# A linear-attention and gated feed-forward kernel: weight loads in three groups, casts moved to GpSimd, a product in two steps, and a new order of the first stage

## The chip, the cores and the metric

The kernel runs on one core of a Trainium2 chip. The metric is the device time of one launch in microseconds (us), median over runs. The engines are TensorE (PE, with its weight loads listed as PEld), VectorE (DVE), ScalarE (ACT), GpSimd (POOL) and SyncE (SP). Here SP issues the loads of the inputs and the stores of the output, GpSimd issues the loads of the weights.

## The reference, cut to what matters

Two operations follow each other. The first is a recurrence over 768 time steps for 4 batches and 8 heads of 48 channels; the second normalises each of the 3072 tokens and applies a gated feed-forward layer with 1536 hidden units.

```python
for t in range(S):                       # S = 768, per batch b and head h
    cur = einsum('bhd,bhe->bhde', u * k_t, v_t)
    y[:, :, t] = einsum('bhd,bhde->bhe', r_t, state + cur)
    state = w_t[..., None] * state + einsum('bhd,bhe->bhde', k_t, v_t)
x = y.transpose(0, 2, 1, 3).reshape(B * S, H * D)        # 3072 x 384
xn = x / sqrt(mean(x * x) + 1e-6) * rms_g
out = (silu(xn @ w_gate) * (xn @ w_val)) @ w_out
```

All inputs and the output are float32. The term with `u` contributes (sum over d of r u k) times v to y; the kernel calls it the bonus.

## The kernel before, in words

Time is cut into 6 superblocks n = 0 to 5 of 128 steps, and in each the 4 batches j = 0 to 3 are handled as blocks of 128 x 384. The recurrence is done in chunks: logarithms of w (`ln`) are summed by a matmul with a triangular matrix (`cs_mm`), exponentials of the sums (`exp_r`, `exp_k`) scale r and k (`r_mul`, `k_mul`) into the tile `rk`; `rk` is transposed (`rk_pe` or a transposing DMA, then `rk_tr`), the products of r and k within the chunk are formed (`q_mm`) and masked (`q_mask_e`, `q_mask_o`), and multiplied with v (`y_mm`), which needs v in bf16 (`cast_v`, tile `vb`). The state is carried by `st_mm` and `st_new` (tile `st`). The bonus runs beside it: `bonus_mul` on GpSimd (r x k x u, two products), `bonus_sum` on VectorE (the sum over a head's channels, tile `diag`), `bonus_v` on GpSimd (times v, tile `ydiag`). In superblock 0 `x_pe` adds `ydiag` into the bank of `y_mm` with a matmul. Then `x_sq`, `x_rstd` and `xn_mul` normalise on ScalarE, `xn_pe` transposes, and `xn_out` on VectorE multiplies by `rms_g` (tile `gT`) into `xnt`.

The feed-forward stage of superblock n works on all 512 tokens at once: for each of 12 blocks f of hidden units, `gate_mm` and `val_mm` (three matmuls of 512 columns each, tiles `wg_sb` and `wv_sb`), `silu` on ScalarE, `h_mul` on VectorE, and finally `o_mm` per batch, `o_out` and `out_dma`. `gate_mm.0.0` is the first such step; it needs all four `xn_out.0.j`.

Every step has a name of the form function.superblock.index. The order is written out by hand in the string `ORDER`: the program calls the functions in that order, so each engine, and each DMA queue, gets its instructions in the order in which their steps stand. An engine works strictly in that order; where a step waits, all behind it on that engine wait. Semaphores between engines follow from the tiles.

The PSUM banks are taken from three rings: "a" (2 banks: sums of `cs_mm`, `gate_mm`), "b" (2 banks: the second sums, `val_mm`), and "q" (4 banks, everything else). `val_mm` thus can't start before the `h_mul` of the value product two before it has read its bank.

In the first stage TensorE has little to do. 13 matmuls on a tile of zeros at the start and 36 steps `warm` among the others fill its time; nothing reads their results. Superblocks 0 and 1 share one load of w (`WIN`). The weights of gate and value are loaded by GpSimd's queue in two groups, hidden blocks 0 to 3 and 4 to 11:

```python
GV = (0, 4, 12)
CAST_ACT = sel("00 01 02 03 10 11 12 13")     # cast_v on ScalarE, else on GpSimd
```

The two products of `bonus_mul` (L467, L468), the casts (L379 on ScalarE, L381 on GpSimd), the weight loads (L351), `xn_out` (L607), the products `r_mul` (L455) and `k_mul` (L461), and the feed-forward products (L626) are the lines that matter below. In superblock 1, `r_mul` and `k_mul` read both operands from SBUF tiles (`er`, `ek`), in superblock 0 one of them from PSUM.

Of the kernel before, what the change touches and what calls it, by code (L numbers as in the profile page):

```python
# [25 lines left out]
load_w.0.1 load_r.0.0 load_w.0.0 warm.4.0 warm.18.0 load_r.0.1 load_k.0.1 load_w.0.2 load_k.0.0 ln.0.1 load_k.0.2  # L26
load_w.0.3 ln.0.0 load_r.0.2 warm.31.0 load_v.0.0 load_v.0.1 warm.22.0 load_k.0.3 load_r.0.3 load_v.0.3 load_v.0.2
cs_mm.0.1 exp_r.0.1 exp_k.0.1 cs_mm.0.0 load_r.1.1 load_k.1.0 load_r.1.0 load_k.1.1 w_tot.0.1 ln.0.2 warm.10.0
load_r.1.3 load_k.1.3 load_r.1.2 load_k.1.2 r_mul.0.1 load_v.1.0 load_v.1.1 load_v.1.2 exp_k.0.0 bonus_mul.0.1
load_v.1.3 load_w.2.0 warm.7.0 exp_r.0.0 k_mul.0.1 bonus_mul.0.0 rk_pe.0.1 w_tot.0.0 warm.2.0 warm.21.0 load_w.2.1  # L30
rk_tr.0.1 warm.9.0 cs_mm.0.2 warm.27.0 bonus_sum.0.1 exp_r.0.2 r_mul.0.0 k_mul.0.0 bonus_mul.0.2 warm.12.0 warm.34.0
warm.13.0 ln.0.3 r_mul.0.2 warm.26.0 rk_pe.0.0 exp_k.0.2 warm.5.0 rk_tr.0.0 load_r.2.1 load_w.2.2 warm.19.0 warm.32.0
cast_v.0.0 cs_mm.0.3 load_r.2.0 load_k.2.0 q_mm.0.1 warm.8.0 w_tot.0.2 k_mul.0.2 bonus_sum.0.0 exp_k.0.3 cs_mm.1.0
bonus_v.0.1 q_mm.0.0 exp_r.0.3 exp_k.1.0 q_mask_e.0.1 q_mask_o.0.1 bonus_sum.0.2 k_mul.0.3 exp_r.1.0 w_tot.0.3
r_mul.0.3 warm.24.0 warm.29.0 rk_pe.0.2 warm.1.0 x_pe.0.1 cast_v.0.1 rk_tr.0.2 y_mm.0.1 bonus_v.0.0 bonus_mul.0.3
q_mask_o.0.0 rk_pe.0.3 q_mask_e.0.0 q_mm.0.2 x_pe.0.0 x_sq.0.1 cast_v.0.3 rk_tr.0.3 q_mask_o.0.2 load_gv.0.0
bonus_sum.0.3 q_mask_e.0.2 cs_mm.1.1 x_rstd.0.1 q_mm.0.3 warm.17.0 bonus_v.0.2 q_mask_o.0.3 y_mm.0.0 warm.25.0
exp_r.1.1 load_w.2.3 x_pe.0.2 load_k.2.1 cast_v.0.2 bonus_v.0.3 warm.20.0 x_sq.0.0 y_mm.0.2 st_mm.0.0 warm.6.0
warm.35.0 xn_mul.0.1 x_rstd.0.0 x_sq.0.2 warm.15.0 q_mask_e.0.3 warm.23.0 x_pe.0.3 xn_mul.0.0 warm.3.0 warm.16.0
y_mm.0.3 exp_k.1.1 cs_mm.1.3 k_mul.1.0 xn_pe.0.1 warm.0.0 bonus_mul.1.0 load_gv.0.1 load_gv.1.0 x_rstd.0.2 warm.30.0  # L40
x_sq.0.3 xn_mul.0.2 r_mul.1.1 st_new.0.0 xn_pe.0.0 r_mul.1.0 warm.14.0 x_rstd.0.3 warm.28.0 warm.33.0 xn_pe.0.2
xn_out.0.1 bonus_mul.1.1 warm.11.0 xn_mul.0.3 exp_k.1.3 xn_out.0.0 st_mm.0.3 xn_out.0.2 st_mm.0.2 xn_pe.0.3 exp_r.1.3
st_new.0.3 cs_mm.1.2 rk_pe.1.0 xn_out.0.3 k_mul.1.1 st_mm.0.1 st_new.0.1 k_mul.1.3 gate_mm.0.0 exp_r.1.2 bonus_sum.1.0
exp_k.1.2 rk_pe.1.1 gate_mm.0.3 rk_tr.1.0 val_mm.0.0 silu.0.0 bonus_sum.1.1 load_gv.1.1 load_r.2.2 bonus_mul.1.3
silu.0.3 val_mm.0.2 rk_tr.1.1 h_mul.0.0 gate_mm.0.2 st_new.0.2 silu.0.2 gate_mm.0.1 bonus_sum.1.3 val_mm.0.3
gate_mm.0.9 silu.0.1 h_mul.0.2 val_mm.0.1 gate_mm.0.6 silu.0.9 r_mul.1.3 h_mul.0.3 q_mm.1.0 h_mul.0.1 silu.0.6
q_mask_e.1.0 q_copy_o.1.0 q_mask_o.1.0 gate_mm.0.11 gate_mm.0.7 q_copy_o.1.1 silu.0.7 rk_pe.1.3 q_mask_e.1.1
q_mask_o.1.1 r_mul.1.2 bonus_v.1.0 val_mm.0.6 val_mm.0.7 cast_v.1.0 k_mul.1.2 rk_tr.1.3 gate_mm.0.5 h_mul.0.6 y_mm.1.0
load_wo.0.0 val_mm.0.9 silu.0.11 bonus_v.1.1 cast_v.1.2 load_wo.1.0 st_mm.1.0 cast_v.1.1 gate_mm.0.4 rk_pe.1.2
h_mul.0.7 st_mm.1.1 silu.0.5 val_mm.0.5 x_add.1.0 rk_tr.1.2 h_mul.0.9 cast_v.1.3 gate_mm.0.10 bonus_mul.1.2 val_mm.0.4  # L50
st_new.1.0 st_new.1.1 load_wo.2.0 q_mm.1.2 h_mul.0.5 silu.0.4 x_sq.1.0 h_mul.0.4 gate_mm.0.8 bonus_v.1.3 q_copy_o.1.3
x_rstd.1.0 q_mask_e.1.3 q_copy_o.1.2 val_mm.0.8 silu.0.8 val_mm.0.11 y_mm.1.1 silu.0.10 q_mask_e.1.2 bonus_sum.1.2
q_mask_o.1.3 h_mul.0.8 x_add.1.1 y_mm.1.3 st_mm.1.2 load_v.2.1 ln.2.0 st_mm.1.3 q_mask_o.1.2 val_mm.0.10 y_mm.1.2
x_sq.1.1 xn_mul.1.0 bonus_v.1.2 cs_mm.2.0 x_add.1.3 x_sq.1.3 st_new.1.2 h_mul.0.11 ln.2.1 h_mul.0.10 x_add.1.2
cs_add.2.0 o_mm.0.0 o_out.0.0 x_rstd.1.1 x_sq.1.2 xn_pe.1.0 xn_out.1.0 xn_mul.1.1 exp_r.2.0 st_new.1.3 cs_mm.2.1
cs_add.2.1 x_rstd.1.2 load_r.2.3 r_mul.2.0 o_mm.0.2 xn_pe.1.1 xn_mul.1.2 xn_pe.1.2 x_rstd.1.3 o_mm.0.1 xn_mul.1.3
bonus_mul.2.0 xn_out.1.1 exp_k.2.0 out_dma.0.0 load_k.2.2 exp_r.2.1 w_tot.2.0 load_v.2.0 ln.2.2 k_mul.2.0 ln.2.3
w_tot.2.1 r_mul.2.1 cs_mm.2.2 xn_pe.1.3 cs_mm.2.3 exp_k.2.1 xn_out.1.2 cs_add.2.2 k_mul.2.1 cs_add.2.3 cast_v.2.1
exp_r.2.2 exp_r.2.3 rk_tr.2.1 xn_out.1.3 o_mm.0.3 exp_k.2.3 o_out.0.1 w_tot.2.2 r_mul.2.2 bonus_mul.2.1 gate_mm.1.7
val_mm.1.7 exp_k.2.2 load_k.2.3 st_mm.2.1 rk_tr.2.0 bonus_sum.2.0 r_mul.2.3 w_tot.2.3 gate_mm.1.1 load_v.2.2 st_new.2.1  # L60
k_mul.2.2 silu.1.7 bonus_mul.2.2 silu.1.1 bonus_sum.2.1 val_mm.1.1 h_mul.1.7 gate_mm.1.6 silu.1.6 bonus_v.2.1
gate_mm.1.5 cast_v.2.0 k_mul.2.3 silu.1.5 rk_tr.2.2 val_mm.1.5 load_w.3.3 o_out.0.2 h_mul.1.1 gate_mm.1.3 gate_mm.1.0
val_mm.1.0 h_mul.1.5 o_out.0.3 silu.1.0 val_mm.1.6 q_mm.2.0 load_v.2.3 q_copy_o.2.0 silu.1.3 q_mask_o.2.0 gate_mm.1.2
st_mm.2.0 h_mul.1.0 val_mm.1.3 rk_tr.2.3 h_mul.1.6 load_w.3.1 load_w.3.0 gate_mm.1.10 val_mm.1.2 load_k.3.1
q_mask_e.2.1 silu.1.2 st_new.2.0 gate_mm.1.4 q_copy_o.2.1 cast_v.2.2 silu.1.4 q_mask_o.2.1 h_mul.1.3 q_mask_e.2.0
y_mm.2.1 y_mm.2.0 h_mul.1.2 st_mm.2.2 bonus_v.2.0 silu.1.10 x_add.2.1 x_add.2.0 gate_mm.1.9 val_mm.1.4 x_sq.2.1
gate_mm.1.8 val_mm.1.9 bonus_mul.2.3 st_new.2.2 out_dma.0.1 x_sq.2.0 h_mul.1.4 load_v.3.2 x_rstd.2.0 silu.1.9 silu.1.8
q_mm.2.2 bonus_sum.2.2 q_copy_o.2.2 h_mul.1.9 gate_mm.1.11 q_copy_o.2.3 out_dma.0.2 load_w.3.2 cast_v.2.3 bonus_v.2.2
bonus_sum.2.3 q_mask_o.2.3 st_mm.2.3 load_k.3.0 q_mask_o.2.2 q_mask_e.2.3 val_mm.1.11 q_mask_e.2.2 val_mm.1.10
bonus_v.2.3 y_mm.2.3 silu.1.11 y_mm.2.2 ln.3.0 h_mul.1.11 h_mul.1.10 x_rstd.2.1 x_add.2.2 ln.3.1 val_mm.1.8 ln.3.3  # L70
h_mul.1.8 cs_mm.3.0 load_r.3.0 x_sq.2.2 xn_mul.2.0 cast_v.3.2 cs_add.3.0 x_add.2.3 exp_k.3.0 x_sq.2.3 o_mm.1.0
cs_mm.3.1 xn_pe.2.0 exp_r.3.0 ln.3.2 x_rstd.2.2 o_mm.1.1 st_new.2.3 load_r.3.1 out_dma.0.3 w_tot.3.0 r_mul.3.0
xn_mul.2.1 k_mul.3.0 xn_mul.2.2 cs_add.3.1 exp_k.3.1 xn_pe.2.2 cs_mm.3.3 x_rstd.2.3 o_out.1.0 exp_r.3.1 bonus_mul.3.1
xn_out.2.2 xn_mul.2.3 o_mm.1.3 w_tot.3.1 xn_pe.2.3 o_out.1.1 cs_add.3.3 r_mul.3.1 load_k.3.2 load_r.3.3 xn_pe.2.1
xn_out.2.0 exp_r.3.3 exp_k.3.3 cs_mm.3.2 xn_out.2.3 o_mm.1.2 load_r.3.2 k_mul.3.1 w_tot.3.3 rk_tr.3.0 r_mul.3.3
cs_add.3.2 out_dma.1.0 xn_out.2.1 load_v.3.0 exp_r.3.2 gate_mm.2.5 exp_k.3.2 r_mul.3.2 w_tot.3.2 val_mm.2.0 gate_mm.2.0
bonus_mul.3.0 bonus_mul.3.2 k_mul.3.2 o_out.1.3 bonus_sum.3.0 silu.2.5 rk_tr.3.1 load_k.3.3 o_out.1.2 q_mm.3.0 silu.2.0
q_mask_e.3.0 val_mm.2.1 bonus_v.3.0 h_mul.2.0 gate_mm.2.1 load_w.4.1 load_v.3.1 load_k.4.3 st_mm.3.2 k_mul.3.3
q_copy_o.3.0 silu.2.1 rk_tr.3.2 load_v.4.0 rk_tr.3.3 val_mm.2.5 gate_mm.2.11 load_k.4.0 bonus_sum.3.1 cast_v.3.0
out_dma.1.1 load_v.3.3 load_w.5.2 q_mask_e.3.1 q_copy_o.3.1 gate_mm.2.2 silu.2.11 h_mul.2.5 val_mm.2.2 h_mul.2.1  # L80
load_w.4.0 gate_mm.2.3 load_v.4.1 silu.2.2 q_mask_o.3.0 cast_v.3.1 load_r.4.1 bonus_sum.3.2 h_mul.2.2 bonus_v.3.1
gate_mm.2.6 val_mm.2.3 y_mm.3.0 st_new.3.2 st_mm.3.0 silu.2.3 gate_mm.2.4 h_mul.2.3 silu.2.6 q_mask_o.3.1 st_new.3.0
st_mm.3.1 silu.2.4 x_add.3.0 load_k.4.1 gate_mm.2.7 val_mm.2.4 x_sq.3.0 gate_mm.2.10 out_dma.1.2 cast_v.4.0 st_new.3.1
val_mm.2.6 q_mm.3.2 h_mul.2.4 bonus_mul.3.3 h_mul.2.6 silu.2.7 val_mm.2.7 val_mm.2.10 load_w.4.3 x_rstd.3.0 silu.2.10
# [640 lines left out]
```

## Time and profile before

| | |
|---|---|
| median of 3 runs | 199.82 us |
| lowest, highest | 199.66, 200.43 us |
| span of the profiled execution | 199.4 us |
| PE, DVE, ACT, POOL busy in it | 194.7, 151.5, 137.1, 125.7 us |
| first feed-forward product (gate_mm.0.0) starts | 31.30 us |
| bytes by DMA, mean rate | 32.41 MB, 163 GB/s |

The profiled execution's own time is its span; the runs' times were taken without a profile and hold 0.4 us more at the median. In the profile a line such as L626 is the line of the kernel that issued an instruction; a row of a timeline has start and duration in us, engine, line, operation, output and inputs, and in brackets how long the engine was idle before it and what ended that. A matmul's duration includes the way through the array, so that successive matmuls overlap; the distance of their starts is what they cost. Busy time of PE includes the filling matmuls. DMA rows give the time from issue to landing.

### The profile page before, as it was taken

The numbers are of one execution on the slowest core, as the hardware profiler recorded it, in microseconds if no ns is written. First come the engines' busy times: TensorE is split into PE (matmuls) and PEld (weight loads), VectorE is DVE, ScalarE is ACT, GpSimd is POOL, SyncE is SP. The second block draws the span as 40 slices with busy tenths as digits, with TensorE's granted clock in tenths as the row PEclk, the third lists the DMA queues.
The fourth block names the chain that finished last, engine by engine and source line by source line (L and its number), as shares of the span: only waits on it lengthen the run. The fifth ranks groups of instructions, "written<-read, shape, count | busy, mean of one in ns | idle before, by whom it ended". The sixth has DMA issues, their size and how long they took to land.

```text
span 199.4 us, 4410 instructions
## 1 busy us (share of the span) xinstructions
PE 194.7 (98%) x1577; PEld 115.6 (58%) x1577; DVE 151.5 (76%) x290; ACT 137.1 (69%) x279; POOL 125.7 (63%) x184
## 2 busy tenths in 40 slices
...
GB/s 147 265 229 191 169 206 208 201 207 191 203 173 212 204 191 227 217 191 191 177 175 226 214 203 215 179 174 139 122 190 219 0 24 60 2 116 82 0 59 100
DMA packets 121566, 32.41 MB, mean 163 GB/s; under 512 B 116420, under 2 KB 120392, under 8 KB 121544
## 3 DMA queue, kind: packets, MB, share of 16 engines
...
q8 instruction: 12, 0.20, 0.4%
...
q10 hardware_dynamic: 8, 0.00, 0.0%
...
## 4 chain that ended last, share of the span: by engine, by line
PE 88%; DMA 5%; DVE 2%; POOL 2%; issue 1%; ACT 0%
PE ps_bu L626 12%; PE ps_av L626 12%; PE ps_au L626 11%; PE ps_bv L626 11%; PE ps_qu L672 7%; PE ps_qz L672 7%; DMA wg_sb<-in_moe_w_gate_dram 5%; PE ps_qx L672 5%; PE ps_qv L672 5%; PE ps_qz L502 1%; PE ps_qx L552 1%; PE ps_qv L502 1%; PE ps_qv L333 1%; PE ps_qu L285 1%; PE ps_qu L502 1%
## 5 line engine op out<-in xcount | busy, mean ns | idle before, releaser
L672 PEld LDWEIGHTS <-ht 128*128 128x128 bf16 x300 | 28.2, 98 | 16.6
L626 PEld LDWEIGHTS <-wg_sb 128*128 128x128 bf16 x216 | 23.1, 114 | 19.8 <-DMA wg_sb<-in_moe_w_gate_dram 0.9
L626 PEld LDWEIGHTS <-wv_sb 128*128 128x128 bf16 x216 | 23.0, 114 | 18.3
L658 DVE TENSOR_TENSOR ht<-ps_bv,sg 128x512 bf16<-128x512 f32 x35 | 24.0, 687 | 10.2 <-PE ps_bv L626 9.1
L658 DVE TENSOR_TENSOR ht<-ps_bu,sg 128x512 bf16<-128x512 f32 x37 | 25.4, 687 | 6.9 <-PE ps_bu L626 5.8
L235 ACT ACTIVATE sg<-ps_av 128x512 bf16<-128x512 f32 x37 | 22.0, 596 | 12.2 <-PE ps_av L626 11.6
L626 PE MATMUL ps_av<-xnt,wg_sb 128*128 128x512 bf16 x111 | 30.1, 380 | 0.0
L626 PE MATMUL ps_bu<-xnt,wv_sb 128*128 128x512 bf16 x111 | 30.1, 380 | 0.0
L626 PE MATMUL ps_au<-xnt,wg_sb 128*128 128x512 bf16 x105 | 28.5, 380 | 0.5 <-DMA wg_sb<-in_moe_w_gate_dram 0.5
L626 PE MATMUL ps_bv<-xnt,wv_sb 128*128 128x512 bf16 x105 | 28.5, 380 | 0.0
L235 ACT ACTIVATE sg<-ps_au 128x512 bf16<-128x512 f32 x35 | 21.0, 600 | 10.5 <-PE ps_au L626 8.7
L467 POOL TENSOR_TENSOR ruk<-rt,kt 128x384 f32<-128x384 f32 x24 | 24.0, 1001 | 6.1 <-DMA kt<-in_k_dram 5.2
L468 POOL TENSOR_TENSOR ruk<-ruk,u_bc 128x384 f32<-128x384 f32 x24 | 24.7, 1030 | 1.9
L520 POOL TENSOR_SCALAR_AFFINE_SELECT qts<-qts 128x512 bf16<-128x512 bf16 x20 | 12.8, 650 | 15.1 <-ACT qts L513 14.6
L477 POOL TENSOR_TENSOR ydiag<-vt,diag 128x384 f32<-128x384 f32 x24 | 20.2, 843 | 1.7 <-DVE diag L472 1.6
L461 POOL TENSOR_TENSOR rk<-kt,ek 128x384 bf16<-128x384 f32 x16 | 15.9, 1004 | 2.3 <-ACT ek L235 2.3
L672 PE MATMUL ps_qu<-wo_sb,ht 128*128 128x384 bf16 (+1 forms) x96 | 15.0, 306 | 0.0
L672 PE MATMUL ps_qz<-wo_sb,ht 128*128 128x384 bf16 x84 | 14.8, 326 | 0.0
L233 ACT ACT_TABLE_LOAD x10 | 12.8, 1283 | 1.8 <-PEq L709 1.6
L472 DVE TENSOR_REDUCE diag<-ruk 128x8 f32<-128x384 f32 x24 | 13.0, 543 | 0.2 <-POOL ruk L468 0.2
L235 ACT ACTIVATE lw<-wt 128x384 bf16<-128x384 f32 (+1 forms) x20 | 11.1, 577 | 2.6 <-DMA wt<-in_w_dram 2.6
L585 ACT ACTIVATE xn<-xb,rstd 128x384 bf16<-128x384 f32 x20 | 11.8, 603 | 0.8 <-POOL rstd L580 0.7
...
## 6 DMA issues: line engine op xcount, KB each, us to landing
rt<-in_r_dram SPq DMA_DIRECT2D x24, 192.0 KB, 4.0
kt<-in_k_dram SPq DMA_DIRECT2D x24, 192.0 KB, 4.2
vt<-in_v_dram SPq DMA_DIRECT2D x24, 192.0 KB, 4.0
out_dram<-ob SPq DMA_DIRECT2D x23, 192.0 KB, 2.3
wt<-in_w_dram SPq DMA_DIRECT2D x16, 192.0 KB, 4.0
wt<-in_w_dram SPq DMA_DIRECT2D x4, 384.0 KB, 4.4
wo_sb<-in_moe_w_out_dram POOLq DMA_DIRECT2D x3, 384.0 KB, 7.0
wg_sb<-in_moe_w_gate_dram POOLq DMA_DIRECT2D x1, 768.0 KB, 10.3
```

What stands on the lines that cost most here:

```text
L233: nc.scalar.preload_act_table_set(table_name)
L235: return nc.scalar.activation(**kw).ins
L461: eng.tensor_tensor(out=rk[:, n % 2, j, 1, :, 0:D], in0=inp["k", n, j], in1=bank["cs_k", n, j][:, 0:DM].rearrange("p (h d) -> p h d", h=H) ...
L467: nc.gpsimd.tensor_tensor(out=ruk[n, j], in0=inp["r", n, j], in1=inp["k", n, j], op=ALU.mult)
L468: nc.gpsimd.tensor_tensor(out=ruk[n, j], in0=ruk[n, j], in1=u_bc, op=ALU.mult)
L472: nc.vector.tensor_reduce(out=diag[n, j].rearrange("p h o -> p (h o)"), in_=ruk[n, j], axis=mybir.AxisListType.X, op=ALU.add)
L477: nc.gpsimd.tensor_tensor(out=ydiag[n, j], in0=inp["v", n, j], in1=diag[n, j].to_broadcast([128, H, D]), op=ALU.mult)
L520: nc.gpsimd.affine_select(out=qts[n, j][:, 1], in_=qts[n, j][:, 1], compare_op=ALU.is_gt, fill=0.0, base=0, pattern=[[0, NP], [1, 128]], c ...
L585: nc.scalar.activation(out=xn, in_=xb[n, j], func=AF.Copy, scale=rstd[n, j][:, 1, c:c + 1])
L626: nc.tensor.matmul(ps[:, cols], lhsT=units(ws, c, f), rhs=xnt[n][:, c, cols], start=(first and c == 0), stop=(c == KC - 1))
L658: nc.vector.tensor_tensor(out=ht[n][:, f, :], in0=bank.pop(("v", n, f)), in1=bank.pop(("sg", n, f)), op=ALU.mult)
L672: nc.tensor.matmul(ps[:, cols], lhsT=ht[n][:, f, b * L:(b + 1) * L], rhs=wo_sb[:, f, cols], start=(f == 0), stop=(f == FC - 1))
```

## The change

It has five parts.

- The weights of gate and value come in three groups of 4 hidden blocks each (`GV = (0, 4, 8, 12)`), six loads instead of four, on the same queue.
- `cast_v` of superblock 0 runs on GpSimd instead of ScalarE.
- `bonus_mul` multiplies r by u first and then by k. The first product is a function `bonus_u`, which in superblock 0 is a step of its own.
- The fill of `st` with zeros is left out. The matmul that spreads u over the partitions and the one that transposes `rms_g` become steps (`u_mm`, `u_out`, `g_mm`, `g_out`) and can be placed.
- The order is new, up to about the fourth superblock; the last 106 steps of PE, 96 of DVE, 110 of ACT, 57 of POOL and 43 of SP are as they were.

Dictionaries for split products (`PARTS`) and for waits between loads (`BEHIND`) are added and left empty.

```diff
-    CAST_ACT = sel("00 01 02 03 10 11 12 13")
+    CAST_ACT = sel("10 11 12 13")
...
     st = persist.tile([128, 2, SB, NP, 2 * D], BF16)
-    nc.vector.memset(st, 0.0)
...
-    GV = (0, 4, 12)
+    GV = (0, 4, 8, 12)
...
+    def u_mm(n, j):
+        bank["u", n, j] = psum("q", ("u", n, j), [128, DM])
+        nc.tensor.matmul(bank["u", n, j], lhsT=ones_row, rhs=u_row, start=True, stop=True)
+
+    def u_out(n, j):
+        nc.vector.tensor_copy(out=u_bc.rearrange("p h d -> p (h d)"), in_=bank.pop(("u", n, j)))
...
+    def bonus_u(n, j):
+        ruk[n, j] = pt.tile([128, H, D], FP32, name="ruk", bufs=NRUK)
+        nc.gpsimd.tensor_tensor(out=ruk[n, j], in0=inp["r", n, j], in1=u_bc, op=ALU.mult)
+
     def bonus_mul(n, j):
-        ruk[n, j] = pt.tile([128, H, D], FP32, name="ruk", bufs=NRUK)
-        nc.gpsimd.tensor_tensor(out=ruk[n, j], in0=inp["r", n, j], in1=inp["k", n, j], op=ALU.mult)
-        nc.gpsimd.tensor_tensor(out=ruk[n, j], in0=ruk[n, j], in1=u_bc, op=ALU.mult)
+        if (n, j) not in ruk:
+            bonus_u(n, j)
+        nc.gpsimd.tensor_tensor(out=ruk[n, j], in0=ruk[n, j], in1=inp["k", n, j], op=ALU.mult)
```

The order of the first stage, per engine, before (-) and after (+):

```diff
 SP
-load_w.0.1 load_r.0.0 load_w.0.0 load_r.0.1 load_k.0.1 load_w.0.2 load_k.0.0 load_k.0.2 load_w.0.3 load_r.0.2 load_v.0.0 load_v.0.1 load_k.0.3 load_r.0.3 load_v.0.3 load_v.0.2 load_r.1.1 load_k.1.0 load_r.1.0 load_k.1.1 load_r.1.3 load_k.1.3 load_r.1.2 load_k.1.2
+load_r.0.0 load_w.0.1 load_w.0.0 load_k.0.1 load_r.0.1 load_w.0.2 load_k.0.2 load_w.0.3 load_k.0.0 load_r.0.2 load_v.0.0 load_v.0.1 load_k.0.3 load_r.0.3 load_r.1.1 load_k.1.0 load_v.0.3 load_v.0.2 load_k.1.3 load_r.1.0 load_k.1.1 load_r.1.3 load_r.1.2 load_k.1.2
 POOL
-bonus_mul.0.1 bonus_mul.0.0 bonus_mul.0.2 bonus_v.0.1 bonus_v.0.0 bonus_mul.0.3 load_gv.0.0 bonus_v.0.2 bonus_v.0.3 bonus_mul.1.0 load_gv.0.1 load_gv.1.0 bonus_mul.1.1 load_gv.1.1 bonus_mul.1.3
+bonus_u.0.1 bonus_u.0.0 bonus_mul.0.1 bonus_mul.0.0 bonus_u.0.2 bonus_mul.0.2 bonus_v.0.1 bonus_v.0.0 cast_v.0.0 bonus_u.0.3 bonus_mul.0.3 cast_v.0.1 load_gv.0.0 bonus_v.0.3 bonus_v.0.2 cast_v.0.3 cast_v.0.2 load_gv.0.1 bonus_mul.1.0 load_gv.1.0 load_gv.2.0 bonus_mul.1.1 load_gv.1.1 load_gv.2.1 bonus_mul.1.3
 DVE, around xn_out of superblock 0
-q_mask_e.0.3 k_mul.1.0 r_mul.1.1 st_new.0.0 r_mul.1.0 xn_out.0.1 xn_out.0.0 xn_out.0.2 st_new.0.3 xn_out.0.3 k_mul.1.1 st_new.0.1 k_mul.1.3 bonus_sum.1.0 bonus_sum.1.1 h_mul.0.0 st_new.0.2 bonus_sum.1.3 h_mul.0.2
+q_mask_e.0.3 r_mul.1.1 st_new.0.0 r_mul.1.0 bonus_sum.1.0 xn_out.0.1 xn_out.0.0 xn_out.0.2 st_new.0.3 xn_out.0.3 k_mul.1.1 st_new.0.2 bonus_sum.1.1 r_mul.1.3 k_mul.1.3 st_new.0.1 h_mul.0.0 bonus_sum.1.3 h_mul.0.2
 PE, around the first feed-forward products
-xn_pe.0.2 warm.11.0 st_mm.0.3 st_mm.0.2 xn_pe.0.3 cs_mm.1.2 rk_pe.1.0 st_mm.0.1 gate_mm.0.0 rk_pe.1.1 gate_mm.0.3 val_mm.0.0 val_mm.0.2 gate_mm.0.2 gate_mm.0.1 val_mm.0.3 gate_mm.0.9 val_mm.0.1
+xn_pe.0.2 cs_mm.1.3 st_mm.0.3 warm.28.0 xn_pe.0.3 rk_pe.1.0 cs_mm.1.2 warm.33.0 st_mm.0.2 st_mm.0.1 gate_mm.0.0 val_mm.0.2 gate_mm.0.3 val_mm.0.0 warm.21.0 rk_pe.1.1 gate_mm.0.2 gate_mm.0.1 warm.11.0 gate_mm.0.9 val_mm.0.3 val_mm.0.1
 PE, the start
-warm.4.0 warm.18.0 warm.31.0 warm.22.0 cs_mm.0.1 cs_mm.0.0
+u_mm.0.0 warm.18.0 warm.2.0 warm.10.0 warm.8.0 warm.31.0 g_mm.0.0 warm.4.0 warm.22.0 cs_mm.0.1 warm.5.0 cs_mm.0.0
```

284 lines of the change are left out of this document (139 added, 145 removed).

## Prediction

> **What bounds the kernel now.** I read the page's engine table first, then busy time by stage, then the chain of waits, then each engine's timeline from 0 to 42 us, then the DMA views. The stage table (columns: stretch in us, PE, PEld, DVE, ACT and POOL busy, granted clock, DMA share, GB/s):
>
> ```profile
> PE 194.7 (98%) x1577; PEld 115.6 (58%) x1577; DVE 151.5 (76%) x290; ACT 137.1 (69%) x279; POOL 125.7 (63%) x184
> ...
> 0.00:31.30 31.30, 30.09 (x257) 18.17 (x258) 21.84 (x46) 22.38 (x50) 22.71 (x34) 1.00 1.00 202
> 31.30:37.00 5.70, 5.23 (x33) 2.79 (x31) 5.28 (x10) 5.25 (x8) 1.37 (x2) 1.00 1.13 204
> 37.00:196.40 159.40, 159.40 (x1291) 94.61 (x1291) 124.33 (x236) 109.11 (x222) 101.57 (x149) 1.00 0.74 155
> ```
>
> From 37 us to the last product TensorE has no gap. The reordering there can open a gap; it has none to close. What can be won lies ahead of 37 us, where busy time deceives, because `warm` matmuls fill it. The real mark is T, the start of gate_mm.0.0, the first product of the feed-forward stage. TensorE's timeline around it:
>
> ```profile
> 29.98 0.49 PE L402 MATMUL ps_av<-lw,mw 128*128 128x384 bf16 x2
> 30.30 0.49 PE L409 MATMUL ps_bu<-lw,mw 128*128 128x384 bf16 x2
> 30.63 0.61 PE L484 MATMUL ps_qz<-ident,rk 128*128 128x128 bf16 x8
> 31.08 0.33 PE L530 MATMUL ps_qu<-vb,rk 128*128 128x96 bf16 x4
> 31.30 0.81 PE L626 MATMUL ps_au<-xnt,wg_sb 128*128 128x512 bf16 x3
> ...
> 36.92 0.84 PE L626 MATMUL ps_au<-xnt,wg_sb 128*128 128x512 bf16 x3 [0.47 <-DMA wg_sb<-in_moe_w_gate_dram]
> ```
>
> T is 31.30 now, and 5 us later TensorE waits 0.47 us for the second gate group. TensorE's real work ahead of T consists of the same steps in both orders (all of superblock 0, cs_mm.1.0 to 1.3, rk_pe.1.0), so also what follows. Hence: new time = old time + (new T - 31.30) + fillers behind T - 0.47 + new waits behind T.
>
> T itself hangs on xn_out, on VectorE. VectorE's timeline:
>
> ```profile
> 7.00 0.56 DVE L334 COPY u_bc<-ps_qv 128x384 f32<-128x384 f32 x1 [2.41 <-PE ps_qv L333]
> 7.48 0.15 DVE L337 COPY gT<-ps_qx 128x3 f32<-128x3 f32 x1
> ...
> 24.45 0.55 DVE L461 TENSOR_TENSOR rk<-kt,ek 128x384 bf16<-128x384 f32 x1
> 24.91 1.35 DVE L455 TENSOR_TENSOR rk<-rt,er 128x384 bf16<-128x384 f32 x1
> ...
> 26.66 2.18 DVE L455 TENSOR_TENSOR rk<-rt,er 128x384 bf16<-128x384 f32 x1
> 28.75 0.55 DVE L607 TENSOR_TENSOR xnt<-ps_qu,gT 128x384 bf16<-128x384 bf16 x1
> 29.22 0.54 DVE L607 TENSOR_TENSOR xnt<-ps_qv,gT 128x384 bf16<-128x384 bf16 x1
> ```
>
> The product r_mul of superblock 1 takes 0.55 us at its cheapest sister (24.45) and 1.35 or 2.18 where GpSimd works beside it; the 2.18 pushes xn_out.0.1 to 28.75. GpSimd's timeline shows what ran beside it:
>
> ```profile
> 13.82 1.00 POOL L467 TENSOR_TENSOR ruk<-rt,kt 128x384 f32<-128x384 f32 x1 [0.92 <-DMA rt<-in_r_dram]
> 14.90 1.00 POOL L468 TENSOR_TENSOR ruk<-ruk,u_bc 128x384 f32<-128x384 f32 x1
> 15.86 0.83 POOL L477 TENSOR_TENSOR ydiag<-vt,diag 128x384 f32<-128x384 f32 x1
> ...
> 24.51 1.34 POOL L468 TENSOR_TENSOR ruk<-ruk,u_bc 128x384 f32<-128x384 f32 x1
> 25.80 0.81 POOL L351 DMA_DIRECT2D wv_sb<-in_moe_w_val_dram  x1
> 26.60 0.77 POOL L351 DMA_DIRECT2D wg_sb<-in_moe_w_gate_dram  x1
> 27.40 1.01 POOL L467 TENSOR_TENSOR ruk<-rt,kt 128x384 f32<-128x384 f32 x1
> ```
>
> **The change part by part.** *State fill.* It goes from VectorE, which sat idle 2.41 us behind it (row 7.00); worth nothing. u_mm and g_mm become steps; g_out moves behind k_mul.0.0, 0.15 us (row 7.48), with no reader before xn_out.0.1.
>
> *Casts.* The four casts of superblock 0 leave ScalarE and join GpSimd:
>
> ```profile
> 16.68 0.52 ACT L379 CAST vb<-vt 128x384 bf16<-128x384 f32 x1
> ...
> 28.45 0.58 ACT L585 ACTIVATE xn<-ps_bu,rstd 128x384 bf16<-128x384 f32 x1
> ```
>
> ```profile
> L381 POOL CAST vb<-vt 128x384 bf16<-128x384 f32 x16 | 8.0, 503 | 0.6 <-DMA vt<-in_v_dram 0.6
> ```
>
> ScalarE sheds 4 x 0.52 = 2.1 us ahead of its last xn_mul (28.45). It keeps only part: on SP load_k.0.0 falls from seventh to ninth place, so k_mul.0.0 and rk_tr.0.0 come later. k.0.0 arrives 2 places later, nearly 2 us at 202 GB/s, and the waiting ScalarE regains part of that; I estimate that 0.8 of the 2.1 us is kept: xn_mul.0.3 ends at 28.2 instead of 29.03.
>
> *Bonus product in steps.* GpSimd's work per block stays two products; r x u can start before k is there. That helps only at the very beginning, where bonus_mul.0.0 then waits for k.0.0. r.0.2 is tenth on SP in both orders with the same bytes ahead, and lands at 13.82 (row); k.0.0, one 192 KB load ahead at 202 GB/s, lands 1.0 earlier: 12.85. From there GpSimd has no gap up to load_gv.0.1. In its new order, pitches from the rows (independent product 0.96, dependent 1.08, bonus_v 0.83, cast 0.50, issue 0.81 to 1.0): bonus_mul.0.0 0.96, bonus .0.2 2.04, two bonus_v 1.66, cast 0.50, bonus .0.3 2.04, cast 0.50, load_gv.0.0 1.0, two bonus_v 1.66, two casts 1.0, load_gv.0.1 0.81: 12.2 us, to 25.05.
>
> Two more moves I price at nothing. Three more fillers stand ahead of cs_mm.0.1 and delay the first exponentials, but k_mul.0.0 waits for k.0.0 anyway; without that cover it is three fillers, 0.5 us at 0.16, on ScalarE's chain. load_v.0.3 and load_v.0.2 go two places back on SP, but GpSimd reads them only after load_gv.0.0, at 21.5.
>
> Then comes bonus_mul.1.0 (both steps), which needs r.1.0, the twentieth load on SP now, the nineteenth before. Issue times and landings of places 19 and 20:
>
> ```profile
> 19.23 0.81 SPq L248 DMA_DIRECT2D rt<-in_r_dram  x1
> 20.09 0.65 SPq L248 DMA_DIRECT2D kt<-in_k_dram  x1
> ```
>
> ```profile
> rt<-in_r_dram SPq DMA_DIRECT2D x1, 192.0 KB, 4.0
> ```
>
> ```profile
> kt<-in_k_dram SPq DMA_DIRECT2D x1, 192.0 KB, 6.3
> ```
>
> Place 20 landed at 26.4 because the first weight group took the engines in between. That group is issued about 0.75 us later now (12.85 + 7.7 = 20.5), so most of place 20 slips through ahead: 24.3 (4.2 after issue) to 26.4; I take 25.3. The two steps, 1.08 + 1.0, and 0.34 for one collision with VectorE (row 24.51, 1.34 against row 14.90's 1.00) give the end of bonus_mul.1.0, B = 27.7 (27.1 to 28.8).
>
> *The new wait.* bonus_sum.1.0 now stands on VectorE directly ahead of xn_out.0.1 and waits for B. Queued behind it are all four xn_out, and behind them TensorE. VectorE: bonus_sum and three xn_out at a pitch of 0.47 bring xn_out.0.2's end to B + 2.0. rk_pe.1.0 takes over its bank, so TensorE follows with rk_pe.1.0 0.45, cs_mm.1.2 0.65, a filler 0.16, two st_mm 0.35: T = B + 3.65 = 31.35, as before within 0.1.
>
> *Fillers and weights behind T.* warm.21 and warm.11 now lie behind T: 2 x 0.16 = 0.33 (half of a 384-column pair, 29.98 to 30.30). val_mm.0.2 needs value group 0 at T + 0.64 = 32.0; issued at 24.2, it has 7.8 us where 384 KB took 6.3:
>
> ```profile
> wg_sb<-in_moe_w_gate_dram POOLq DMA_DIRECT2D x1, 384.0 KB, 6.3
> ```
>
> ```profile
> q0 software_dynamic: 143, 0.15, 86.2%
> ```
>
> gate_mm.0.9 now reads group 2, issued second at B + 0.8. It is due after six products of 0.64 (three matmuls of 512 columns each, where 384 take 0.16), rk_pe.1.1's 0.45 and the fillers: T + 4.6 = 36.0. Group 1 lands 6.3 after B, group 2 needs 0.39 MB more at 0.15 MB per us (row of GpSimd's queue for one us), 2.6: 36.6; less a little since the last of 6.3 is latency, 36.4. Stall 0.4 (0 to 2.0, the latter if the pair takes the 10.3 us from 26.60 to 36.92, as the old 768 KB did). The other groups are due 9 us and more behind T and covered.
>
> Sum: T +0.05, fillers +0.33, old stall -0.47, new stall +0.4 = +0.3. The profiled span is 199.4, 0.4 below the median of 199.82, which I take as what lies around it: **200.1 us**. Its own range, from B's bounds and the stall's, is 199.1 to 201.2.
>
> **The rivals.**
>
> *Slower: VectorE's products are shut out.* Behind xn_out.0.3 VectorE has k_mul.1.1, r_mul.1.3 and k_mul.1.3, which read two SBUF tensors each, ahead of h_mul.0.0 and h_mul.0.2, whose banks TensorE needs for val_mm.0.3 and 0.1. In the old order GpSimd falls idle just then (1.37 of 5.70 us in the stage table); now it is busy to B + 7.4 (four issues, two bonus pairs). One h_mul takes 0.69:
>
> ```profile
> L658 DVE TENSOR_TENSOR ht<-ps_bv,sg 128x512 bf16<-128x512 f32 x35 | 24.0, 687 | 10.2 <-PE ps_bv L626 9.1
> ```
>
> With p for each product, h_mul.0.2 ends at B + 2.85 + 3p + 3 x 0.47 (two st_new, bonus_sum.1.1) + 0.69 + 0.47 (bonus_sum.1.3) + 0.69 = B + 6.1 + 3p. TensorE is at val_mm.0.1 at T + 5.9 = B + 9.6, 10.0 with the stall. So it decides from p = 1.3 on. At one GpSimd product waited out (1.0 + 0.55) it costs 0.75: 200.9; at row 26.66's 2.18 each it costs 2.6: 202.7. For it: both dear rows. Against it: not all three need meet a long instruction.
> The Trainium skill, "SBUF — State Buffer", section "Who interferes with whom", says that a VectorE instruction with two SBUF inputs and a GpSimd one that reads SBUF exclude each other, the later waiting the earlier out. By that rule p is at most 1.55; row 26.66 (2.18) is longer, so here VectorE waited for two, and the measurement decides.
>
> *Slower: r.1.0 late.* If place 20 lands at 26.4 again, B is 28.8, T 32.45: +1.4, 201.2 us. For it: the weight group still comes from the same engine at nearly the same time. Against it: the 0.75 us.
>
> *Faster: GpSimd is sooner.* If k.0.0 lands well ahead of 12.85 and products don't collide, B is no limit, and T follows xn_mul.0.3: 28.2 + transposes 0.2 + the 1.65 of TensorE's steps = 30.1. Then T -1.2, fillers +0.33, old stall -0.47: 198.5 us. It needs B at 26.4, below my lower bound; my walk can be off by that.
>
> That the change does nothing there (casts off a ScalarE that was not last) is within the forecast.
>
> **How the numbers follow.** Forecast 0.36, shut-out products 0.23, late r.1.0 0.17, sooner GpSimd 0.24. A measurement of this kernel tells about 0.5%, 1.0 us: faster means below 198.8, slower above 200.8. Of the forecast 0.30 lies within and 0.06 above; shut-out 0.04 and 0.19; late r.1.0 0.02 and 0.15; sooner GpSimd 0.04 within and 0.20 below. Faster 0.20, same 0.40, slower 0.40. The range runs from the fast rival's 198.5 to just short of the 2.18 price, 202.3.
>
> **What would show it.** Right: bonus_sum.1.0 waits on GpSimd just ahead of xn_out.0.1 at about 27.7; T near 31.4; a wait of TensorE for the third gate group near 36; PE without gaps from 43 us on. Wrong: xn_out.0.1 before 26.5 (the fast rival); gaps of TensorE at 36 to 42 ended by VectorE (first rival); GpSimd waiting for DMA rt near 25 (second); any gap after 43 us, which I price at nothing.

## Result and the profile after

The changed kernel takes 203.33 us (median of 4 executions, 202.91 to 203.42), the kernel before 199.78 beside it (199.66 to 200.43): a ratio on record of 1.014, 95% interval 1.0097 to 1.0183 (the two medians alone give 1.018). It is slower by 3.55 us where the forecast was +0.3, and the time lies above the range, which ended at 202.3. Later comparisons were made on other chips, where the kernel before took 201.0 to 201.7; so kernels are compared by their ratios to the kernel before on the same chip; executions over 1.5% above the fastest of their kernel are left out of these.

The page's engine line and the stage table of the changed kernel, in the columns of before:

```profile
PE 192.4 (96%) x1557; PEld 114.4 (57%) x1577; DVE 148.6 (74%) x289; ACT 136.6 (68%) x275; POOL 128.7 (64%) x190
```

```profile
0.00:31.30 31.30, 26.69 (x237) 15.61 (x238) 18.90 (x44) 20.40 (x43) 22.57 (x36) 0.95 0.99 197
31.30:37.00 5.70, 5.65 (x47) 3.63 (x46) 5.67 (x10) 4.46 (x8) 4.94 (x6) 1.00 1.23 207
```

Twenty matmul records are missing (1557 against 1577 weight loads), so small holes in PE's share behind 37 us are not read. What can be read is T, on TensorE's timeline, and the wait for the third gate group behind it:

```profile
29.86 0.33 PE L604 MATMUL ps_qv<-ident,xn 128*128 128x128 bf16 x3 [0.50 <-DVE xnt L615]
...
32.77 0.81 PE L634 MATMUL ps_au<-xnt,wg_sb 128*128 128x512 bf16 x2
...
37.73 0.84 PE L634 MATMUL ps_av<-xnt,wg_sb 128*128 128x512 bf16 x3
```

T is 32.77 instead of 31.30, and from 29.86 to T TensorE has no gap: it was released by VectorE's first xn_out. Ahead of that stand, on VectorE:

```profile
26.76 1.14 DVE L459 TENSOR_TENSOR rk<-rt,er 128x384 bf16<-128x384 f32 x1
28.79 0.55 DVE L480 TENSOR_REDUCE diag<-ruk 128x8 f32<-128x384 f32 x1 [0.89 <-POOL ruk L476]
29.26 0.55 DVE L615 TENSOR_TENSOR xnt<-ps_qv,gT 128x384 bf16<-128x384 bf16 x1
```

That is the new wait of the forecast, bonus_sum.1.0 on GpSimd, 0.89 us long. What GpSimd did:

```profile
13.79 1.00 POOL L476 TENSOR_TENSOR ruk<-ruk,kt 128x384 f32<-128x384 f32 x1 [2.55 <-DMA kt<-in_k_dram]
...
19.31 1.00 POOL L471 TENSOR_TENSOR ruk<-rt,u_bc 128x384 f32<-128x384 f32 x1 [0.47 <-DMA rt<-in_r_dram]
...
22.80 1.99 POOL L485 TENSOR_TENSOR ydiag<-vt,diag 128x384 f32<-128x384 f32 x2
...
27.56 1.20 POOL L476 TENSOR_TENSOR ruk<-ruk,kt 128x384 f32<-128x384 f32 x1
28.71 1.57 POOL L345 DMA_DIRECT2D wg_sb<-in_moe_w_gate_dram  x2
```

It waits twice for loads, and bonus_mul.1.0, whose end the prediction calls B, ends at 28.76 (27.56 + 1.20). ScalarE, which sheds four casts, is later, not sooner:

```profile
10.42 0.84 ACT L237 ACTIVATE lw<-wt 128x768 bf16<-128x768 f32 x1 [2.90 <-DMA wt<-in_w_dram]
...
29.65 0.58 ACT L593 ACTIVATE xn<-ps_bu,rstd 128x384 bf16<-128x384 f32 x1
```

The last xn_mul ends at 30.23, against 29.03 before. ln.0.2 waits 2.90 us for w.0.2, and in the new order the first exponentials are queued behind it, but that is made up again: the fourth copy of rk_tr starts sooner than before. The loss comes behind it, by way of TensorE. First the changed kernel, then the kernel before:

```profile
21.00 1.01 ACT L501 COPY rkT<-ps_qz 128x1024 bf16<-128x1024 bf16 x1 [0.41 <-PE ps_qz L492]
21.88 0.36 PE L560 MATMUL ps_bu<-vb,qts 128*128 128x48 bf16 x8 [0.59 <-POOL vb L385]
24.84 0.91 PE L565 MATMUL ps_av<-ydiag,ident 128*128 128x384 f32 x2 [0.26 <-ACT ek L237]
```

```profile
21.52 1.01 ACT L493 COPY rkT<-ps_qz 128x1024 bf16<-128x1024 bf16 x1
20.79 0.84 POOL L477 TENSOR_TENSOR ydiag<-vt,diag 128x384 f32<-128x384 f32 x1
```

At 21.88 a y_mm has waited for a cast of v, now on GpSimd. At 24.84 x_pe.0.2 reads the product of bonus_v.0.2, which GpSimd ends at 24.79 (22.80 + 1.99), against 21.63 before; the exponential of ScalarE that the row names ends at the same moment. From there TensorE has no gap up to y_mm.0.3 at 28.08, and ScalarE's steps up to the last xn_mul follow at once.

Between the two profiled executions the span grows by 1.8 (199.4 to 201.2). The sum in the prediction's form, T +1.47, fillers +0.33, old stall -0.47, new stall +0.3 (37.43 to 37.73), gives +1.6. The other 1.7 us of the medians is in neither trace; the first experiment bears on it.

### The profile page after: what moved, and what is told of

Its sections match the earlier page's. It is cut to its first block, busy times and chain, and to the rows that moved or that the text cites. A ratio compares the mean times of both kernels' runs of the same rounds, so it can differ in the third digit from the quotient of the medians.

```text
span 201.2 us, 4382 instructions
## 1 busy us (share of the span) xinstructions
PE 192.4 (96%) x1557; PEld 114.4 (57%) x1577; DVE 148.6 (74%) x289; ACT 136.6 (68%) x275; POOL 128.7 (64%) x190
## 4 chain that ended last, share of the span: by engine, by line
PE 79%; POOL 7%; DMA 6%; SPq 4%; issue 2%; ACT 0%; POOLq 0%
PE ps_bv L634 12%; PE ps_au L634 11%; PE ps_av L634 11%; PE ps_bu L634 11%; PE ps_qv L675 8%; PE ps_qx L675 7%; PE ps_qz L675 5%; DMA wg_sb<-in_moe_w_gate_dram 4%; PE ps_qu L675 4%; DMA kt<-in_k_dram 2%; SPq L266 2%; SPq L253 2%; POOL ydiag L485 2%; POOL ruk L476 2%; POOL ruk L471 2%
## 5 line engine op out<-in xcount | busy, mean ns | idle before, releaser
L660 DVE TENSOR_TENSOR ht<-ps_bv,sg 128x512 bf16<-128x512 f32 x37 | 25.4, 686 | 11.1 <-PE ps_bv L634 8.5
L634 PE MATMUL ps_bv<-xnt,wv_sb 128*128 128x512 bf16 x105 | 29.5, 380 | 0.3
L634 PE MATMUL ps_av<-xnt,wg_sb 128*128 128x512 bf16 x106 | 29.2, 380 | 0.2
L660 DVE TENSOR_TENSOR ht<-ps_bu,sg 128x512 bf16<-128x512 f32 x35 | 24.0, 686 | 7.3 <-PE ps_bu L634 6.9
L634 PE MATMUL ps_bu<-xnt,wv_sb 128*128 128x512 bf16 x97 | 27.7, 380 | 0.5
L471 POOL TENSOR_TENSOR ruk<-rt,u_bc 128x384 f32<-128x384 f32 x24 | 24.2, 1012 | 5.1 <-DMA rt<-in_r_dram 5.0
L476 POOL TENSOR_TENSOR ruk<-ruk,kt 128x384 f32<-128x384 f32 x24 | 24.4, 1015 | 4.3 <-DMA kt<-in_k_dram 2.6
L675 PE MATMUL ps_qv<-wo_sb,ht 128*128 128x384 bf16 x96 | 16.9, 326 | 0.0
L675 PE MATMUL ps_qx<-wo_sb,ht 128*128 128x384 bf16 x84 | 14.8, 326 | 0.0
L578 ACT ACTIVATE junk<-xb 128x384 bf16<-128x384 f32 x20 | 10.4, 521 | 4.4 <-DVE xb L569 4.0
```

Of the source, the lines that this page charges most:

```text
L471: nc.gpsimd.tensor_tensor(out=ruk[n, j], in0=inp["r", n, j], in1=u_bc, op=ALU.mult)
L476: nc.gpsimd.tensor_tensor(out=ruk[n, j], in0=ruk[n, j], in1=inp["k", n, j], op=ALU.mult)
L578: nc.scalar.activation(out=junk, in_=xb[n, j], func=AF.Square, accum_out=rstd[n, j][:, 0, c:c + 1])
L634: nc.tensor.matmul(ps[:, cols], lhsT=units(ws, c, f), rhs=xnt[n][:, c, cols], start=(c == 0), stop=(c == KC - 1))
L660: nc.vector.tensor_tensor(out=ht[n][:, c, cols], in0=bank.pop(("v", n, f))[:, cols], in1=bank.pop(("sg", n, f))[:, cols], op=ALU.mult)
L675: nc.tensor.matmul(ps[:, cols], lhsT=ht[n][:, f, b * L:(b + 1) * L], rhs=wo_sb[:, f, cols], start=(f == 0), stop=(f == FC - 1))
```

## Experiments

**Both kernels again.** Unchanged; this gives second traces, and spans beside times.

> The kernel before, unchanged, profiled again. The prediction took the time outside the span as 0.4 us (199.82 less 199.4); in the runs since, each time is 1.70 us over its span, so the execution that was profiled before (199.4) was itself about 1.3 us longer than the median one (198.1). Theory 1, what varies is the landing of the second gate group and T with it: this trace shows T at 30.5 to 31.3 and a stall for the gate weights between 0 and 1.3 us. Theory 2, something behind 43 us varies: gaps of TensorE there.

Ratio 0.9998 (0.9953 to 1.0043). The profiled execution took 201.14 for a span of 199.4: 1.7 us lie around a span, not 0.4, in every run of this case that has both numbers. A span of 199.4 thus belongs to a time of 201.1, 1.3 us above the median of 199.82 that the prediction started from, if that trace was taken on the same chip, which the record does not say. By the list of TensorE's waits of this trace (from 27 us):

```profile
PE ps_au L626 <- DMA wg_sb<-in_moe_w_gate_dram: 1.1, 1, 1.1
PE ps_qx L672 <- DMA wo_sb<-in_moe_w_out_dram: 0.6, 1, 0.6
```

T (from here on the first weight load of gate_mm.0.0) is 29.82 here, below theory 1's bounds, and was 31.27 in the trace that the prediction used; the stall for gate weights is 1.05 instead of 0.47. Both theories hold in part: T and the landing vary, and w_out stalls an o_mm at 54 us for 0.6. Over the eight traces of the old head in this case T was 29.5 to 31.3, median 30.2 (in the four with an unaltered head, before, b0, h2 and g1, 29.8 to 31.3, median 30.7): the prediction's trace was at the late end.

> The changed kernel, unchanged, profiled again on the chip of its parts. Theory 1, all the loss is ahead of 43 us: T near 32.8, a stall of 0.3 for the third gate group, no gap behind. Theory 2, the new order also leaves the transposes of superblock 3 no margin (a wait of 1.1 and 1.8 us for rkT near 105 us in two of its relatives, 0.1 in one): such a wait shows here in some size from 0 to 1.8.

202.86, 206.42 and 208.60 us: there is no ratio, and the trace, of the longest, stands only as a sign: T 32.88, a wait of 1.0 for gate weights, and one of 2.4 for rkT, as theory 2 has it. The next two runs bear on the same wait.

**The order cut in two at o_mm.0.0.**

```diff
-ORDER = new
+ORDER = new up to o_mm.0.0, then the remaining steps in the old order     # h1
-ORDER = old
+ORDER = old up to o_mm.0.0, then the remaining steps in the new order     # h2
```

> The changed kernel's steps up to o_mm.0.0 in their new order, the rest in the order of the kernel before. Theory 1, the head alone costs: as the changed kernel unchanged. Theory 2, the new order behind it costs as well (the wait for rkT in superblock 3): no wait for rkT near 105 us here, and faster than the changed kernel by the size of that wait, 0.1 to 1.8 us.

> The kernel before up to o_mm.0.0, the rest in the new order. Theory 1, the head alone costs: as the kernel before. Theory 2, the new order behind it costs as well: slower than the kernel before by 0.1 to 1.8 us, with a wait of TensorE for rkT near 104 us in the trace.

New head with old tail: 1.0051 (1.0004 to 1.0097). Old head with new tail: 1.0181 (1.0104 to 1.0257). So the new order loses time behind o_mm.0.0 too, at 53 us, where the prediction had priced nothing, and of the two halves that is the larger here. The halves do not add up to the 1.014 of the whole, and in the changed kernel's own first trace all of the loss lies ahead of 43 us; its other three executions are about 0.5 us from that one at most. TensorE's waits of the second:

```profile
PE ps_qz L502 <- DMA rkT<-rk: 2.4, 1, 2.4
...
PE ps_qu L502 <- DMA rkT<-rk: 0.6, 1, 0.6
```

q_mm.3.2 waits at 105.5 for rk_tr.3.3, the last DMA transpose of superblock 3. SP's queue in that kernel, and below it in the kernel before:

```profile
96.67 1.83 SPq L489 DMA_TRANSPOSE rkT<-rk  x1
98.55 0.58 SPq L261 DMA_DIRECT2D wt<-in_w_dram  x1
99.17 1.80 SPq L248 DMA_DIRECT2D kt<-in_k_dram  x2
101.09 1.58 SPq L489 DMA_TRANSPOSE rkT<-rk  x1
```

```profile
92.98 1.62 SPq L489 DMA_TRANSPOSE rkT<-rk  x1
94.64 0.58 SPq L248 DMA_DIRECT2D vt<-in_v_dram  x1
95.34 1.79 SPq L489 DMA_TRANSPOSE rkT<-rk  x1
```

Three loads instead of one stand between the last two transposes, and the last is issued 5.75 us later, 3.4 us after the product of GpSimd that it reads was done. That product (k_mul.3.3) is later too, before and then in this kernel:

```profile
93.70 1.00 POOL L461 TENSOR_TENSOR rk<-kt,ek 128x384 bf16<-128x384 f32 x1
```

```profile
96.73 1.00 POOL L461 TENSOR_TENSOR rk<-kt,ek 128x384 bf16<-128x384 f32 x1
```

And the landing takes longer: 3.7 us before, up to 6.7 here (the transposes of 93 to 108 us, tile rkT):

```profile
DMA to landing us min/median/max: 3.7/3.7/3.7
```

```profile
DMA to landing us min/median/max: 3.3/3.7/6.7
```

Before, it landed at 99.0, and q_mm.3.2 ran at 103.2: 4 us to spare. In the new order it landed at 107.8. In the first trace of the changed kernel it was issued at 99.82 and landed 5.3 us later, at 105.1; its reader came at 105.3. That this trace shows no loss behind 43 us hangs on 0.2 us.

**One place of the tail.** In the changed kernel, and in the old head with the new tail:

```diff
-rk_tr.3.2 load_w.4.1 load_k.4.0 load_k.4.2 rk_tr.3.3     (SP)
+rk_tr.3.2 rk_tr.3.3 load_w.4.1 load_k.4.0 load_k.4.2
```

> The changed kernel with one step of SP's queue moved: rk_tr.3.3 directly behind rk_tr.3.2, ahead of load_w.4.1, load_k.4.0 and load_k.4.2. In the runs of the new tail it was issued at 99.8 to 101.1 and landed at 105.2 to 107.8, and TensorE waited 0 to 2.4 us for it near 105; its last product on GpSimd is done at 96.7 to 97.7. Theory 1, its place on SP is the cause: it is issued near 98, lands by 103, TensorE has no wait for rkT, and the time falls to that of the new head with the old tail (203.1), 1 to 3 us under the changed kernel on this chip. Theory 2, k_mul.3.3 on GpSimd is late for itself: the wait stays above half of its size.

> The kernel before up to o_mm.0.0, the new order behind it, with rk_tr.3.3 directly behind rk_tr.3.2 on SP's queue. Without that last edit it was 1.8% slower than the kernel before (3.6 us), with waits of 2.38 us near 105 and 0.59 near 96 for transposes. Theory 1, the place on SP carries it: the wait near 105 goes, the slowdown falls to 0.3 to 1.0 us (0.6 for the wait near 96). Theory 2, the new tail is late as a whole: the wait near 105 shrinks by less than half or turns up at another step, and the kernel stays more than 1.2% slower.

Changed kernel with it: 1.0117 (1.0026 to 1.0207). The interval holds both the 1.014 of the changed kernel and the 1.0051 of the new head with the old tail, so the time tells nothing; in the trace TensorE has no wait for rkT. Old head with it: 1.0102 (1.0072 to 1.0133), where it was 1.0181. SP's queue and TensorE's waits of the latter:

```profile
95.64 3.38 SPq L489 DMA_TRANSPOSE rkT<-rk  x2
```

```profile
PE ps_bv L626 <- DVE ps_bu L425: 0.8, 1, 0.8
...
PE ps_qu L502 <- DMA rkT<-rk: 0.4, 1, 0.4
```

The wait near 105 is gone, so the place on SP causes that wait. Of the new tail's slowdown it carries a little under half by the two ratios (their intervals overlap, 1.0104 to 1.0133); the rest has waits of its own, 0.4 for the first transpose of the superblock and 0.8 near 120 us for VectorE. So neither theory is right alone. Those two were not taken apart.

**Parts of the head, undone one at a time in the changed kernel.**

```diff
-bonus_sum.1.0 xn_out.0.1 xn_out.0.0 xn_out.0.2 st_new.0.3 xn_out.0.3     # u1, VectorE
+xn_out.0.1 xn_out.0.0 xn_out.0.2 st_new.0.3 xn_out.0.3 bonus_sum.1.0
-load_k.0.2 load_w.0.3 load_k.0.0                                         # u2, SP
+load_k.0.0 load_k.0.2 load_w.0.3
-CAST_ACT = sel("10 11 12 13")                                            # u3
+CAST_ACT = sel("00 01 02 03 10 11 12 13")
```

> The changed kernel with one step of VectorE moved: bonus_sum.1.0 behind xn_out.0.3 instead of directly ahead of xn_out.0.1. In the changed kernel it waits for GpSimd until 28.79 us, xn_out.0.1 starts at 29.26 and T (the first gate product) is 32.77. Theory 1, the wait alone sets T: xn_out.0.1 starts at 27.9, right behind r_mul.1.0, T falls by 1.36 to 31.4, and the kernel by 1.4 us. Theory 2, ScalarE is late as well (its last xn_mul ends at 30.23, 1.2 later than in the kernel before): T cannot come before 30.23 + 0.16 + 1.6 = 32.0, and the kernel gains 0.75 us at most. Theory 3, the head is not what costs: no change.

T falls to 31.05, by 1.7 and more than either theory said. But bonus_mul.1.0 (27.74) and the last xn_mul (29.21) end 1.0 us sooner in this trace as well, which the move does not explain; about 0.7 is left for the move itself, as theory 2 has it. The time does not follow as far as can be seen: the four executions took 202.88 to 206.97 us, too far apart for a ratio, and the span of the trace is 201.2, as that of the changed kernel was on another chip. TensorE's row for gate_mm.0.9:

```profile
37.53 0.84 PE L634 MATMUL ps_av<-xnt,wg_sb 128*128 128x512 bf16 x3 [1.62 <-DMA wg_sb<-in_moe_w_gate_dram]
```

It starts at 37.53, as against 37.73: an earlier T turned into a longer wait for the third gate group.

> The changed kernel with load_k.0.0 back in seventh place on SP's queue, as in the kernel before. GpSimd waited 2.55 us for it, until 13.79. Theory 1, this late load pushes the whole chain of GpSimd: the end of bonus_mul.1.0 (28.76) moves up by about 1 us and so does T. Theory 2, GpSimd has a second wait behind it (0.47 us for r.0.3, until 19.31), which takes the gain back: bonus_mul.1.0 stays at 28.8 and T within 0.3 us of 32.77.

Theory 2: k.0.0 is used at 11.17 instead of 13.79, GpSimd then waits 2.05 for r.0.2, 0.49 for r.0.3 and 0.63 for r.1.0, bonus_mul.1.0 ends at 29.09, T is 33.07. Ratio 1.0148 (1.0083 to 1.0212).

> The changed kernel with the four casts of superblock 0 back on ScalarE (GpSimd loses 4 x 0.5 us ahead of bonus_mul.1.0, ScalarE gets 4 x 0.5 us ahead of its last xn_mul). Theory 1, GpSimd's chain through bonus_mul.1.0 sets T: three casts of it stand behind the wait at 19.31, so B falls by 1.5 to 27.3 and T by about 1.4, the time too. Theory 2, ScalarE's chain is equally late: its last xn_mul goes from 30.23 to 31.0 or later (idle of 1.2 us ahead of it takes up part), T to 32.8 or more, the time the same or up to 1 us worse.

bonus_mul.1.0 ends at 27.36 and T falls to 31.88, as theory 1 said in direction; but the time is 1.0195 (1.0125 to 1.0266), with 0.7 us of waiting for gate weights and 1.8 for rkT. With waits for rkT of 0 to 2.4 us, runs of the new tail cannot show a gain of 1 us in the head. The last xn_mul ends at 30.04, hardly sooner than 30.23: bonus_v.0.2 is done at 23.82, but x_pe.0.2 then starts at 24.66, behind an exponential of ScalarE, which has its casts again. Theory 2's 31.0 did not come.

**Parts of the change alone in the kernel before.**

```diff
-GV = (0, 4, 12)                                            # p1; f3 also loads 2.0 ahead of 1.0
+GV = (0, 4, 8, 12)
-xn_out.0.1                                                 # g2, VectorE
+bonus_sum.1.0 xn_out.0.1
-CAST_ACT = sel("00 01 02 03 10 11 12 13")                  # g3
+CAST_ACT = sel("10 11 12 13")
```

> The kernel before with one part of the change alone: gate and value weights in three groups, the third issued directly behind the second, everything else as before. The first product that needs a group beyond the first is gate_mm.0.9, which now needs the third group: 0.39 MB behind the second as before, plus one more issue. So the stall at 36.92 stays or grows from 0.47 to about 0.8 us: 199.8 to 200.2. If splitting were worth something by itself the stall would be gone: 199.3. Its span beside its time also shows what lies outside the span in kernels of the old order.

1.0033 (0.9991 to 1.0075), stall 1.3: the split alone does nothing that can be told.

> The kernel before with three groups, and the third group, which gate_mm.0.9 needs first, loaded ahead of the second. Theory 1, the stall at 35 to 37 us (0.47 to 1.3) goes and nothing takes its place: 0.5 to 1 us faster than the kernel before. Theory 2, the second group is due 1.3 us later and lands where the large group did, so 0 to 0.8 us of stall comes back there, or the run gives the time back at o_mm.0.0 to w_out: within 0.5 us of the kernel before.

1.0032 (0.9994 to 1.007). The stall is down to 0.22, but 0.85 comes back at 42.3, where TensorE waits for a cast of v on ScalarE, and that for a load of v that came 2.2 us late. So the time stays, as theory 2 has it, but at another place than it named.

> The kernel before with one step of VectorE moved: bonus_sum.1.0 directly ahead of xn_out.0.1, as in the changed kernel. Its bonus_mul.1.0 ends at 29.7, so xn_out.0.1 starts at about 30.2 instead of 26.8 to 28.8, and T comes 1.4 to 3 us later. Theory 1, TensorE's order sets the time: slower by that, 1.4 to 3 us. Theory 2, the second gate group lands at 36.2 to 36.9 anyway and TensorE waits for it 0.5 to 1.1 us now, so that much of the later T is hidden: slower by 0.5 to 2 us, and the wait for the gate weights is gone.

1.0002 (0.9978 to 1.0027). The expectation read the wrong row: the pair that ends at 29.7 is bonus_mul.1.1; bonus_mul.1.0 ends at 25.85 there (row 24.51 of the prediction), before VectorE comes to it. So the place of bonus_sum.1.0 costs nothing by itself; in the changed kernel's first trace it costs because GpSimd is 2.9 us later.

> The kernel before with one part of the change alone: the four casts of superblock 0 on GpSimd, order as before. ScalarE loses 2.1 us ahead of its last xn_mul, GpSimd gets 2.0 ahead of load_gv.0.1 and load_gv.1.0. Theory 1, GpSimd's transfers are the tighter side: the second gate group is issued at 28.6 instead of 26.6, lands near 38.5, and TensorE waits about 2 us for it instead of 0.5 to 1.1: 1 to 1.5 us slower. Theory 2, ScalarE was the tighter side: T up to 1 us earlier and the time 0 to 0.5 us better.

1.0044 (1.0009 to 1.0079): theory 1, at the lower end. T is 30.10, within the spread of the unaltered head, and the gate weights are late:

```profile
PE ps_au L626 <- DMA wg_sb<-in_moe_w_gate_dram: 1.9, 1, 1.9
```

The casts alone are a loss of about 0.9 us. By this one trace it goes through the weight transfers that GpSimd issues behind them: the second gate group is issued at 27.35 instead of 26.60. The bonus product in steps, the missing fill and the new order of the loads were not tried alone.

**Repairs together.** u1's move with load_gv.2.0 ahead of load_gv.1.0: on top of f1 (f2), and on the new head with the old tail (f4).

> The changed kernel with rk_tr.3.3 early, bonus_sum.1.0 behind xn_out.0.3, and the third gate group loaded ahead of the second. Theory 1, these three places are the whole loss: T falls to about 31.0, the wait for the gate weights (1.6 us with bonus_sum.1.0 moved alone) goes, since the group that is needed first lands 2.4 us sooner, the wait for rkT goes; 1.5 us under the kernel with rk_tr.3.3 early alone, and about level with the kernel before (201.2 here, within 0.5). Theory 2, the next transfer takes over (the second gate group at 38, w_out at o_mm.0.0): the gain over the kernel with rk_tr.3.3 alone is under 0.5 us.

> The new head with the old tail (203.1, +0.5%), with bonus_sum.1.0 behind xn_out.0.3 and the third gate group ahead of the second. Theory 1, the head's loss is the wait of bonus_sum.1.0 and the group's landing: T 32.3 to 31.0, the stall of 1.1 us goes, 1.5 to 2.4 us faster, so up to 1 us under the kernel before. Theory 2, transfers bound the stage from 35 to 54 us whatever the order: o_mm.0.0 starts at the same 54 us and the time is within 0.7 us of 203.1.

f4: 1.0025 (0.9994 to 1.0057), T 31.23, no wait for gate weights: the new head repaired is level with the old one, not better. f2: 1.0151 (1.006 to 1.0241), T 33.02, worse than expected, although VectorE no longer waits for bonus_sum.1.0. In f2 and f1 k_mul.1.0 on VectorE is long, and masks that y_mm needs stand behind it; VectorE and GpSimd in f1:

```profile
21.96 2.72 DVE L465 TENSOR_TENSOR rk<-kt,ek 128x384 bf16<-128x384 f32 x1
```

```profile
22.20 1.63 POOL L485 TENSOR_TENSOR ydiag<-vt,diag 128x384 f32<-128x384 f32 x2
23.76 1.28 POOL L385 CAST vb<-vt 128x384 bf16<-128x384 f32 x2
```

A product with two SBUF inputs takes 2.72 us instead of 0.55, and ends behind both bonus_v and the first cast of GpSimd. The Trainium skill, "SBUF — State Buffer", section "Who interferes with whom", has the two engines lock each other out over a shared pair of ports; the trace agrees, but here VectorE sat out three instructions. k_mul.1.0 took 0.73 to 0.81 in the changed kernel's first trace, u1, h1 and f4, and 1.8 to 2.7 in a0, u2, u3, f1 and f2. f2 and f4 have the same head: T 33.02 with 2.72 us, 31.23 with 0.81; half of that difference, 0.9, is there already when k_mul.1.0 starts (22.66 and 21.77). With it short and bonus_sum.1.0 moved (u1, f4) T was 31.05 and 31.23; in all other traces of the new head 31.9 to 33.1. No version tried beats the kernel before.

## Why the prediction was wrong

Two steps failed. The first is T = B + 3.65 = 31.35, "as before within 0.1": T was 32.77. B came 1.06 later than forecast, and from B to T it took 4.0 us instead of 3.65, because the first xn_out released TensorE, not the third, and more steps stood between it and T. Of the 3.2 us between 200.1 and 203.33 that is 1.4. Another 1.7 comes from putting one trace beside the median of other executions: the one profiled before was 1.3 us above its median by b0's count, that of the changed kernel 0.4 below its own. About 0.2 stays open.

The second is "From 37 us to the last product TensorE has no gap. The reordering there can open a gap; it has none to close", which then went into the sum as nothing. The steps behind 43 us were not walked, and their margins not worked out. The trace of before showed the one that mattered: SP issued rk_tr.3.3 at 95.3, 8 us ahead of its reader, and the new order puts two more loads ahead of it and GpSimd's k_mul.3.3 two to three us later. In the changed kernel's first trace the price of nothing held, with 0.2 us to spare; in a0, u2, u3 and h2 the wait was 1.1 to 2.4 us. By the runs of halves the new tail alone costs 1.8%, the head 0.5%.

The terms of the head, one by one:
- *T = 31.35* was 32.77, and 32.3 to 32.9 in the other traces of the unaltered new head, against 29.8 to 31.3 in the unaltered old one. Between the medians of these, 32.6 and 30.7, the head's delay is 1.8 us, not 0.05, and part of it is hidden: the old head then waits up to 1.1 us for gate weights.
- *B = 27.7* was 28.76: k.0.0 was there at 13.79 instead of 12.85, r.0.3 cost a wait of 0.47 that the walk did not have, and two bonus_v took 1.99 instead of 1.66.
- *ScalarE keeps 0.8 of 2.1 us* was wrong in sign: the last xn_mul ended at 30.23, not 28.2. The shed time was spent waiting for TensorE, which stood behind GpSimd's casts and bonus_v. With the casts back (u3) the end is 30.04, so the casts alone are not the reason.
- *New stall 0.4 (0 to 2.0)*: 0.3, and 0.4 to 1.1 in f1, a0 and h1. The estimate held, and in u1 it grew to 1.6 when T came sooner.
- *Fillers +0.33* and *state fill nothing* were not contradicted.
- *0.4 us lies around the span* was wrong (1.7), since the span of one execution was subtracted from the median of others. It hid the 1.3 us above.

What T hung on is narrower than the forecast's path. In thirteen of the seventeen traces, of both orders, T comes 1.8 to 1.9 us behind the end of the last xn_mul; that is the fast rival's form (0.2 + 1.65), not B + 3.65. bonus_sum.1.0 waits for GpSimd ahead of xn_out in two traces alone, the changed kernel's first and u2, where T comes 2.5 and 2.7 behind xn_mul; in the kernel before (2.2) and a0 (2.1) VectorE was late without such a wait. So most of the later T came by way of xn_mul, and the new wait that the forecast rested on was worth about 0.7 us.

The rivals: "shut out" was priced at products behind xn_out.0.3 and has no gap of TensorE there. The same mechanism shows at k_mul.1.0, ahead of xn_out, though it is not all: h1 had k_mul.1.0 at 0.73 us and T at 32.28. "Late r.1.0" named the B that came (28.8) with a cause that did not: GpSimd did not wait for r.1.0 in the first trace (it did in u2, for 0.63, and B was 29.09). "GpSimd sooner" did not come.

In fifteen of the seventeen traces, old and new, span less T less TensorE's waits behind T comes out at 167.6 to 168.9 us, so T and the waits carry the differences. The exceptions are u3 (170.1, at a granted clock of 0.98) and a0 (170.4, at 0.99).
